# First values of the forward scans: one reciprocal of twelve columns for three limited ones of four, and the copy for the check on ScalarE

## The chip, the cores and the metric

The kernel runs on one core of a Trainium2 chip. The metric is the device time of one execution in microseconds. Engines are named as in the profile: PE (TensorE, matrix products), DVE (VectorE), ACT (ScalarE), POOL (GpSimd) and SP, whose queue issues most of the DMA transfers. An engine works through its own instructions in order; where it needs a result of another engine it waits on a semaphore.

## The reference

A gated linear attention feeds a SoLU block. All data are float32 except the weights of the second block, which come as float64.

```python
B, H, S, D = 4, 8, 768, 48
for t in range(S):
    state = alpha[:, :, t, :, None] * state + einsum('bhd,bhe->bhde', k[:, :, t], v[:, :, t])
    y[:, :, t] = einsum('bhd,bhde->bhe', q[:, :, t], state)
x = y.transpose(0, 2, 1, 3).reshape(3072, 384)
h = x @ w_in                          # 384 x 1024
solu = h * softmax(h)
ln = (solu - mean) / sqrt(var + 1e-6) * g_ln
out = ln @ w_out                      # 1024 x 384
```

alpha lies between 0.8 and 1.0.

## The kernel before

**Groups.** The sequence is cut into G = 6 groups of 128 positions; a group holds all four batches (512 tokens). In each group the attention is computed in chunk form: for position s within a group, the products of alpha up to and from s are put into q and k, so that scores, masked values and the state become matrix products.

**Layout.** For these products alpha, q and k lie with features on partitions: 32 rows per batch, and 12 column blocks (NB = 12): eight blocks, one for each head's first 32 features, and four for the last 16 features of two heads each. A block of alpha has 129 columns (SW = P + 1), the first of which is a zero that separates one block's scan from the next. The 12 blocks are worked in three parts of four (NP = 4, part i = 0, 1, 2; part 2 holds the last features).

**The scans.** Both run on DVE as tensor_tensor_scan (line 220), with state = data0 * state + data1.

- `scan_back(g, i)` runs backward over a part of aT with `unit` (1 in the first column of a block, else 0) and writes hT: the products of alpha from a position to the group's end. Column 1 of a block is then the product over the whole group.
- `scan_on(g, i)` runs forward over a part of aT, in place, with `seed`, which has the inverse of that whole product in the first column of a block and zeros elsewhere. It yields the factors that belong to q.

Before the change, every `scan_on` first limits the four whole products from below by LEAST = 1e-13 into `least` (line 234), takes their reciprocals into a seed tile (line 235) and scans. There are two seed tiles, taken by i % 2. With i = 2, which is the first of a group's three, the 12 whole products are also copied by DVE to `fend` (line 231); at the end of the kernel fend is compared with LEAST, and where any is below, a general path is run instead of this one.

**Who reads the results.** hT is read by the products for keys (kT: by DVE in lines 685 and 762 for groups 0 and 1, by POOL in line 244 from group 2 on) and by `decay` on POOL (line 264). The forward scan's aT is read by the products for queries (qe, qv: lines 693, 772, 780 on DVE; line 255 on POOL from group 2 on). ACT multiplies qe by a parity mask into the second half of qv (`apart`, line 248). The scores (line 282) need kT and both halves of qv; DVE masks them (line 293); the results y (line 314) are copied by ACT to x (line 351).

**The second block.** For each of eight pieces f of 128 features: three accumulated products h (line 389) on PE, exponential on ACT (403), h * e on DVE (404), square on ACT (405), running sums p on POOL and DVE (420). The down projection o (line 500) of one group is interleaved with the attention of a later one; `finish` (517 to 533) forms the row factors with DVE and POOL and writes out.

**Order.** The order of instructions is written out by hand (`tc.manual_schedule()`), and a tile framework places the semaphores. Group 0 and 1 have an order of their own: group 0's transposes are made by PE, and the float64 weights are fetched into a room of slots (`fetch`, line 564, 16 transfers for two pieces of w_in) and unpacked to float32 by DVE (`bits`, lines 594 to 606) beside it. In group 1's attention the three `scan_on` are spread between finish(0) and the query products. Group 2's first two scans stand before group 1's second block, its third in the step behind piece 1 (plan `first`, entry `on1`). For groups 3 to 5 all three stand behind piece 1 of the second block of the group two before:

```python
behind={0: "states v keys", 1: "load on2 on0 on1", 2: "lasts firsts", 3: "apart", 5: "decay", 6: "alpha", 7: "back"},
```

`ps_a` has four PSUM banks of one buffer each, through which transposes, scores, y and the sums pass in turn; `ps_h` and `ps_o` have two each.

Of the kernel before, what the change touches and what calls it, by code (L numbers as in the profile page):

```python
# [9 lines left out]
FP = mybir.dt.float32  # L10
# [4 lines left out]
ALU = mybir.AluOpType  # L15
AX = mybir.AxisListType
P = 128
# [15 lines left out]
def fast_path(ctx, tc, q, k, v, alpha, moe_w_in, moe_w_out, moe_g_ln, out):  # L33
# [12 lines left out]
    nc = tc.nc  # L46
# [5 lines left out]
    NP = H // 2  # L52
    NB = H + NP
# [5 lines left out]
    LEAST = 1e-13  # L59
    PS = bass.MemoryType.PSUM  # L60

    def pool(name, bufs, **kw):
        return ctx.enter_context(tc.tile_pool(name=name, bufs=bufs, **kw))

    const = pool("const", 1)
# [3 lines left out]
    small = pool("small", 4)  # L69
# [27 lines left out]
    fend = const.tile([P, G, NB], FP, name="fend")  # L97
# [19 lines left out]

    SW = P + 1
    aT = const.tile([P, NB, SW], FP, name="aT")
    seed = [const.tile([P, NP, SW], FP, name=f"seed{i}") for i in range(2)]  # L120
    unit = const.tile([P, NP, SW], FP, name="unit")
    hT = const.tile([P, NB * SW + 2], FP, name="hT")
    h4 = hT[:, 0 : NB * SW].rearrange("p (j s) -> p j s", s=SW)
# [92 lines left out]
    def scan(out, data, start, flip):  # L216
        a, o, s = (x.rearrange("p j s -> p (j s)") for x in (data, out, start))
        if flip:
            a, o, s = a[:, ::-1], o[:, ::-1], s[:, ::-1]
        nc.vector.tensor_tensor_scan(out=o, data0=a, data1=s, initial=1.0, op0=ALU.mult, op1=ALU.add)  # L220
# [5 lines left out]

    def scan_on(g, i):
        part = slice(NP * i, NP * i + NP)
        s = seed[i % 2]
        if i == 2:  # L230
            nc.vector.tensor_copy(out=fend[:, g], in_=h4[:, :, 1])

        least = small.tile([P, NP, 1], FP, name="least")
        nc.vector.tensor_scalar(out=least, in0=h4[:, part, 1:2], scalar1=LEAST, scalar2=None, op0=ALU.max)  # L234
        nc.vector.reciprocal(out=s[:, :, 0:1], in_=least)
        scan(aT[:, part], aT[:, part], s, False)

    def keys_T(g):
        firsts(kn, kT[:, 0:H])
# [414 lines left out]
    nc.gpsimd.memset(unit[:, :, 0:1], 1.0)  # L654
    nc.gpsimd.memset(aT[:, :, 0:1], 0.0)
    nc.gpsimd.memset(hT[:, NB * SW : NB * SW + 2], 1.0)
    for s in seed:
        nc.gpsimd.memset(s, 0.0)
    nc.gpsimd.memset(state, 0.0)
    load_v_first(0)  # L660
    fetch(0, 3, 2)
# [18 lines left out]
    turned(kn, ends_of(kn), t)  # L680
    alpha_over(0)
    scan_on(0, 2)
    for i in range(3):
        part = slice(NP * i, NP * i + NP)
        nc.vector.tensor_tensor(out=kT[:, part], in0=t[i], in1=hk[:, part], op=ALU.mult)
    scan_on(0, 0)
    t = three("tp_q", [(ps_o, "o"), (ps_o, "o"), (ps_a, "a0")])
    turned(qn, ends_of(qn), t)
    for i in (2, 0, 1):
        if i == 1:  # L690
            scan_on(0, i)
        part = slice(NP * i, NP * i + NP)
        nc.vector.tensor_tensor(
            out=qe if i == 2 else qv[:, part], in0=t[i], in1=aT[:, part, 1:SW], op=ALU.mult
        )
        if i == 2:
            apart()
# [61 lines left out]
    for i in range(3):  # L759
        scan_back(1, i)  # L760
        part = slice(NP * i, NP * i + NP)
# [15 lines left out]
    for i in range(2):  # L777
        scan_on(1, i)
        part = slice(NP * i, NP * i + NP)
# [150 lines left out]
    def compare(out, x, bound, op):  # L930
# [6 lines left out]
        out=chunks[:, :, 2], in0=sums[:, :, 2], scalar=0.25, in1=sums[:, :, 3], op0=ALU.mult, op1=ALU.is_le  # L937
# [6 lines left out]
    else:  # L944
# [9 lines left out]
        out=bad, in0=all_ok[0:1, 0:1], scalar1=float(P * ends[-1]), scalar2=None, op0=ALU.is_lt  # L954
# [415 lines left out]
def kernel(tc, *args):  # L1370

    with ExitStack() as ctx:
        taken = fast_path(ctx, tc, *args)
    with tc.If(taken > 0):
        general_path(tc, *args)
# [30 lines left out]
```

## Time and profile before

| What | Value |
|---|---|
| Time, median of 7 runs | 391.03 us (389.18 to 394.36) |
| Time of the profiled execution | 390.95 us |
| Span of the profiled execution, first to last instruction | 389.0 us |
| Mean granted TensorE clock in it | 0.991 of full |
| DVE busy, instructions | 250.4 us, 417 |
| ACT busy, instructions | 144.1 us, 252 |
| Forward scans (aT from aT and seed) | 18, 23.0 us |
| least / seed reciprocal / fend copy | 18, 6.5 us / 18, 3.2 us / 6, 2.4 us |

In a row of the timeline stand the start in us from the span's start, the duration in us, the engine, the line of the kernel, the operation, output and inputs with their shape, and the count; in brackets the idle time of the engine just before and what ended it. Rows of a pipelined engine overlap a little. In the list of waits stand the total in us, how often, and the longest. A chain of waits goes back from the last instruction to what released it.

### The profile page before, as it was taken

To read this page: it belongs to the slowest core of one execution; us is meant where nothing else is said; L and a number is where in the kernel's file an instruction comes from. 1 tells how busy PE (TensorE), PEld (TensorE's weight loads), DVE (VectorE), ACT (ScalarE), POOL (GpSimd) and SP (SyncE) were. 2 spreads that over 40 slices of the span, in tenths; PEclk is the share of its full clock that TensorE was granted. 3 is DMA by queue.
4 is the path that set the end of the run, shared out by engine and by line. 5 is a ranking of instruction groups with operands and counts; after the bars stand their busy time and mean duration, and the time that the engine had idled before them with its cause. 6 is when DMAs were issued, how large, how long until landed. Compare 5 with 4: busy or idle time off the path is not lost.

```text
span 389.0 us, 10598 instructions
## 1 busy us (share of the span) xinstructions
PE 371.5 (95%) x4661; PEld 224.4 (58%) x4661; DVE 250.4 (64%) x417; ACT 144.1 (37%) x252; POOL 125.6 (32%) x135
## 2 busy tenths in 40 slices
PE   8798999787999999999999999999999999999995
PEld 8685345455665556656556556566555675555552
DVE  0989889996987767793755893665895511444410
ACT  2528775553425325225153225253123231333111
POOL 4020000041032992337413436422635620333210
PEclk9989999999899999999999999999999999999999
DMA  9975989303446300764000763000600000000011
GB/s 186 193 195 152 235 269 163 93 20 86 111 109 87 83 4 2 111 155 102 22 3 22 117 151 100 22 3 22 103 0 22 22 24 2 20 21 21 22 43 48
DMA packets 86567, 30.79 MB, mean 79 GB/s; under 512 B 68072, under 2 KB 84720, under 8 KB 86512
## 3 DMA queue, kind: packets, MB, share of 16 engines
q1 hardware_dynamic: 85488, 29.11, 34.5%
q10 hardware_dynamic: 1024, 0.92, 0.7%
q8 instruction: 38, 0.62, 0.7%
q14 instruction: 17, 0.14, 0.1%
HBM read 25.30 MB, written 4.72 MB: 77 GB/s over the span
## 4 chain that ended last, share of the span: by engine, by line
PE 71%; DVE 12%; SPq 5%; ACT 5%; DMA 4%; issue 2%; ACTq 0%; DVEq 0%
PE o L500 30%; PE h L389 24%; PE y L314 9%; PE a L282 5%; SPq L564 2%; DMA room<-in_moe_w_in_dram 2%; SPq L152 2%; DVE room L404 2%; PE kv L364 1%; ACT sq L581 1%; DVE aT L220 1%; DMA kn<-in_k_dram 1%; DVE top L597 1%; DVE sT L293 1%; DVE hT L220 1%
## 5 line engine op out<-in xcount | busy, mean ns | idle before, releaser
L500 PE MATMUL o<-w_out,room 128*128 128x385 f32 x384 | 135.2, 496 | 1.0 <-DVE least L234 1.0
L389 PE MATMUL h<-x,w_in 128*128 128x512 f32 x288 | 132.2, 598 | 1.3 <-DVE g_col L618 1.2
L500 PEld LDWEIGHTS o<-w_out,room 128*128 128x128 f32 x384 | 72.0, 191 | 58.2 <-issue 16.1
L389 PEld LDWEIGHTS h<-x,w_in 128*128 128x128 f32 x288 | 53.0, 189 | 59.9 <-issue 48.7
L404 DVE TENSOR_TENSOR room<-h,e 128x512 f32<-128x512 f32 x40 | 27.7, 692 | 82.7 <-ACT e L403 82.5
L403 ACT ACTIVATE e<-h 128x512 f32<-128x512 f32 x40 | 23.9, 598 | 104.9 <-PE h L389 104.9
L530 POOL TENSOR_TENSOR r<-sums,mhalf 128x1 f32<-128x1 f32 x20 | 14.3, 716 | 138.6 <-DVE sums L522 138.6
L420 POOL TENSOR_TENSOR p<-p,e 128x512 f32<-128x512 f32 x30 | 41.7, 1391 | 15.7 <-ACT e L403 15.7
L405 ACT ACTIVATE u<-room 128x512 f32<-128x512 f32 x40 | 25.2, 631 | 42.2 <-DVE room L404 42.2
L293 DVE TENSOR_TENSOR sT<-a,mask 128x512 f32<-128x512 f32 x44 | 27.3, 682 | 9.9 <-PE a L282 8.9
L282 PE MATMUL a<-qv,kT 32*128 32x128 f32 x704 | 27.5, 288 | 4.4 <-DVE least L234 2.2
L282 PEld LDWEIGHTS a<-qv,kT 32*128 32x128 f32 x704 | 24.0, 195 | 11.9 <-issue 4.3
L220 DVE TENSOR_TENSOR_SCAN hT<-aT,unit 128x516 f32<-128x516 f32 x18 | 23.0, 1329 | 8.8 <-ACT aT L677 8.7
L420 DVE TENSOR_TENSOR p<-p,u 128x512 f32<-128x512 f32 x30 | 23.1, 771 | 6.5 <-ACT u L405 6.5
L244 POOL TENSOR_TENSOR kT<-kT,hT 128x1024 f32<-128x1024 f32 (+1 forms) x8 | 13.3, 1684 | 43.0 <-DVE kT L195 43.0
L314 PE MATMUL y<-sT,vn 128*32 128x128 f32 x768 | 23.6, 274 | 1.1 <-DVE sT L293 0.5
L220 DVE TENSOR_TENSOR_SCAN aT<-aT,seed 128x516 f32<-128x516 f32 x18 | 23.0, 1277 | 0.6
L314 PEld LDWEIGHTS y<-sT,vn 128*32 128x32 f32 x768 | 20.9, 110 | 3.3 <-issue 2.4
L212 ACT ACTIVATE sq<-an,mone 128x1536 uint8<-128x1536 f32 x12 | 18.8, 1570 | 0.2
L314 PE MATMUL y<-qv,state 32*32 32x128 f32 x960 | 16.8, 277 | 1.0 <-DVE sT L293 0.9
L314 PEld LDWEIGHTS y<-qv,state 32*32 32x32 f32 x960 | 12.1, 103 | 7.9 <-issue 5.4
L532 ACT ACTIVATE o_sb<-o,r 128x384 f32<-128x384 f32 x16 | 9.3, 582 | 18.8 <-POOL r L530 15.6
(141 smaller groups left out, 379.6 us busy)
## 6 DMA issues: line engine op xcount, KB each, us to landing
an<-in_alpha_dram SPq DMA_DIRECT2D x20, 192.0 KB, 4.9
out_dram<-o_sb SPq DMA_DIRECT2D x20, 192.0 KB, 1.9
room<-in_moe_w_out_dram SPq DMA_DIRECT2D x8, 384.0 KB, 4.8
kn<-in_k_dram SPq DMA_DIRECT2D x16, 192.0 KB, 4.1
qn<-in_q_dram SPq DMA_DIRECT2D x16, 192.0 KB, 3.8
vn<-in_v_dram SPq DMA_DIRECT2D x10, 256.0 KB, 3.9
room<-in_moe_w_in_dram SPq DMA_DIRECT2D x16, 128.0 KB, 4.3
kn<-in_k_dram SPq DMA_DIRECT2D x4, 384.0 KB, 5.8
```

Source lines behind the costliest of these rows:

```text
L212: nc.scalar.activation(out=sq, in_=x, func=AF.Relu, scale=sign, bias=mone, accum_out=over[:, g, i : i + 1])
L220: nc.vector.tensor_tensor_scan(out=o, data0=a, data1=s, initial=1.0, op0=ALU.mult, op1=ALU.add)
L282: nc.tensor.matmul(a[b][:, i], lhsT=kT[quarter(b), kb], rhs=qv[quarter(b), qb], start=kb == h, stop=kb != h, tile_position=(32 * b, 0), sk ...
L293: nc.vector.tensor_tensor(out=sT[:, b, half * NP : half * NP + NP], in0=a[b], in1=mask[:, None, :].to_broadcast([P, NP, P]), op=ALU.mult,)
L314: nc.tensor.matmul(y_bank(b)[quarter(r), a], lhsT=lhsT, rhs=rhs, start=(b, r) not in begun, stop=stop, tile_position=(row, 32 * r), skip_g ...
L389: nc.tensor.matmul(h, lhsT=w_in[:, a, f * P : (f + 1) * P], rhs=d["x"][:, a].rearrange("p b t -> p (b t)"), start=(a == 0), stop=(a == KC ...
L403: nc.scalar.activation(out=e, in_=h, func=AF.Exp)
L404: nc.vector.tensor_tensor(out=u, in0=h, in1=e, op=ALU.mult)
L405: nc.scalar.activation(out=u2, in_=u, func=AF.Square)
L420: eng.tensor_tensor(out=p, in0=d[0][i] if f == 1 else p, in1=d[f][i], op=ALU.add)
L500: nc.tensor.matmul(d["o"][:, 0 : DM + 1], lhsT=u_of(g, f)[:, b * P : b * P + P], rhs=w_out[:, f], start=(f == 0), stop=(f == FC - 1), skip ...
L530: nc.gpsimd.tensor_tensor(out=r, in0=s[:, 3:4], in1=mhalf, op=ALU.pow)
```

## The change

The two seed tiles of four blocks become one of twelve. With i = 2, ahead of the group's first forward scan, one reciprocal takes all 12 whole products from hT, without the limit, and writes the first columns of all blocks of the seed; the copy to fend is made by ACT instead of DVE. The scans read their part of the seed. The comparison of fend with LEAST at the end stays. On POOL the seed is cleared by one memset in place of two.

```diff
-    seed = [const.tile([P, NP, SW], FP, name=f"seed{i}") for i in range(2)]
+    seed = const.tile([P, NB, SW], FP, name="seed")
...
     def scan_on(g, i):
         part = slice(NP * i, NP * i + NP)
-        s = seed[i % 2]
         if i == 2:
-            nc.vector.tensor_copy(out=fend[:, g], in_=h4[:, :, 1])
-
-        least = small.tile([P, NP, 1], FP, name="least")
-        nc.vector.tensor_scalar(out=least, in0=h4[:, part, 1:2], scalar1=LEAST, scalar2=None, op0=ALU.max)
-        nc.vector.reciprocal(out=s[:, :, 0:1], in_=least)
-        scan(aT[:, part], aT[:, part], s, False)
+
+            nc.vector.reciprocal(out=seed[:, :, 0:1], in_=h4[:, :, 1:2])
+            nc.scalar.copy(out=fend[:, g], in_=h4[:, :, 1])
+        scan(aT[:, part], aT[:, part], seed[:, part], False)
...
-    for s in seed:
-        nc.gpsimd.memset(s, 0.0)
+    nc.gpsimd.memset(seed, 0.0)
```

The order of instructions on PE, POOL and SP is the same but for the memset. On DVE 42 instructions go and 6 come; on ACT 6 come: in group 0 behind the two passes over alpha (line 212), in group 1 behind the copies of kg (line 303), in group 2 behind the second passes over alpha and ahead of the x copies, in groups 3 to 5 behind o_sb (line 532).

## The prediction

> **What bounds the kernel now.** I read the page first: its engine rows, then the chain that ended last.
>
> ```profile
> PE 371.5 (95%) x4661; PEld 224.4 (58%) x4661; DVE 250.4 (64%) x417; ACT 144.1 (37%) x252; POOL 125.6 (32%) x135
> PE 71%; DVE 12%; SPq 5%; ACT 5%; DMA 4%; issue 2%; ACTq 0%; DVEq 0%
> ```
>
> TensorE is busy 95% of the span and holds 71% of the chain. Since an average hides stages, I next took the list of waits of PE. From 150 to 389 us it is empty: PE runs through. All its waits lie earlier, and these four are on steps that the touched scans feed (columns: us in total, times, longest):
>
> ```profile
> PE a L282 <- DVE least L234: 2.2, 1, 2.2
> PE a L282 <- DVE qv L780: 1.5, 1, 1.5
> PE a L282 <- ACT qv L248: 0.3, 1, 0.3
> PE a L282 <- POOL qv L255: 0.2, 1, 0.2
> ```
>
> So only time saved in groups 0, 1 and 2 (before about 137 us) can reach the end. Groups 3 to 5 have the same DVE instructions, but there PE is the bound.
>
> **What is removed.** Group rows of DVE by line: the six fend copies are 2.4 us busy, the 18 limits (least) 6.5 us, the 18 reciprocals 3.2 us: 12.1 us. Six reciprocals of 12 columns come in. The trace has none: the row of 4 columns is 180 ns. Lower bound 0.18. Upper: the Trainium skill, "VectorE: DVE Perf Modes", section "First, the fixed hardware budget", runs reciprocal as an iterated divide with a repeat count of 8; 8 more columns at 8 cycles of the page's 0.96 GHz are 67 ns, an estimate of 0.25. By the rows, fend with 12 columns (168 ns) against the copy of 1 column (154) says columns cost little; I take 0.19. The difference is 0.06 a group, three times: 0.2 at most. DVE loses about 11 us of busy time in all. What of it counts must be read from three places.
>
> **Group 1 (80 to 88.6 us)** is the cleanest. The DVE timeline there:
>
> ```profile
> 80.26 0.16 DVE L231 COPY fend<-hT 128x12 f32<-128x12 f32 x1
> 80.33 0.17 DVE L234 TENSOR_SCALAR least<-hT 128x4 f32<-128x4 f32 x1
> 80.53 0.18 DVE L235 RECIPROCAL seed<-least 128x4 f32<-128x4 f32 x1
> 80.75 1.23 DVE L220 TENSOR_TENSOR_SCAN aT<-aT,seed 128x516 f32<-128x516 f32 x1
> ...
> 83.67 0.16 DVE L234 TENSOR_SCALAR least<-hT 128x4 f32<-128x4 f32 x1
> 83.87 0.18 DVE L235 RECIPROCAL seed<-least 128x4 f32<-128x4 f32 x1
> 84.09 1.33 DVE L220 TENSOR_TENSOR_SCAN aT<-aT,seed 128x516 f32<-128x516 f32 x1
> ...
> 86.06 0.24 DVE L234 TENSOR_SCALAR least<-hT 128x4 f32<-128x4 f32 x1
> 86.33 0.18 DVE L235 RECIPROCAL seed<-least 128x4 f32<-128x4 f32 x1
> 86.55 1.29 DVE L220 TENSOR_TENSOR_SCAN aT<-aT,seed 128x516 f32<-128x516 f32 x1
> ```
>
> Instructions that need nothing of the one before start 0.08 before its end; dependent ones 0.02 to 0.03 after it. First scan: the reciprocal runs 80.26 to 80.45, the scan starts at 80.47 instead of 80.75: 0.28. Second and third need no step of their own: 83.68 for 84.09 is 0.41, 86.06 for 86.55 is 0.49. Sum 1.18. The scores of PE start at 88.62, 0.04 after the last qv product (L780), which frees their bank; the down projection ahead of them ends at 86.7, so PE can follow by the whole amount. Late next would be the alpha of group 2 (the SP queue issues it after the ACT pass over alpha, itself after o_sb and a POOL power): I expect it some 0.6 earlier only, but DVE has idle time of 1.3 and 2.0 us before its products at 115.9 and 119.7, which covers it. **1.2 us.**
>
> **Group 0 (13 to 28 us).** By the same counting the three scans start 0.36, 0.76 and 1.23 earlier, PE's scores (19.76) 0.76 earlier, and the masks with them. Behind the eight masks DVE unpacks the first weights (L594, at 27.79), and these need all 16 transfers of the first fetch. The chain shows the issues: the sixteenth at 24.93; its landing takes 2.4 us: 27.33. So from there on DVE gains 27.79 - 27.33 = 0.46 and no more. The second fetch (issued until 33.6, landing about 2.5 later) is needed at 37.4 and doesn't cap further. **0.45 us.** Lower end 0, if the landing moves; upper end 0.76, if it comes earlier.
>
> **Group 2 (119 to 137 us).** On the path is only the third scan; the other two (110 to 113.6) lie ahead of DVE's idle 1.3 us. Here a rule speaks against the plain sum. The rows:
>
> ```profile
> 119.71 1.28 POOL L420 TENSOR_TENSOR p<-e 128x512 f32<-128x512 f32 x1 [4.98 <-ACT e L403]
> 120.27 0.74 DVE L234 TENSOR_SCALAR least<-hT 128x4 f32<-128x4 f32 x1
> 121.04 0.18 DVE L235 RECIPROCAL seed<-least 128x4 f32<-128x4 f32 x1
> 121.26 1.23 DVE L220 TENSOR_TENSOR_SCAN aT<-aT,seed 128x516 f32<-128x516 f32 x1
> ```
>
> The limit took 0.74 instead of its usual 0.16 and ended with POOL's product (120.99). Taken as its own price, limit and reciprocal give back 0.97. But the Trainium skill, "SBUF — State Buffer", section "Who interferes with whom", says that a DVE instruction with two SBUF inputs also blocks behind a GpSimd instruction that reads SBUF. The scan has two (aT and seed), and the row at 110.24 agrees: a scan of 1.88 us while POOL multiplied keys until 111.02. Then the scan, moved to 120.3, waits until 120.99 itself and ends at about 122.2 instead of 122.49. I follow rule and row: **0.3 us**, upper end 0.9. PE could use up to its waits of 0.2 + 0.3 us at 128 to 129 and part of the stall of the scores at 133.8.
>
> **What is added.** The fend copy on ACT: ACT rows near it are 0.19 (128x1) and 0.24 apiece (the state copies of 128x192, four in 0.96); I take 0.2. It is queued behind the two passes over alpha in group 0 (ACT free at 15.2; next is the copy of q's ends, which PE needs at 16.4: 0.5 to spare), ahead of the pair of products by parity in group 1 (ends at about 85, PE needs it at 87.4), and behind o_sb in groups 3 to 5, where ACT idles 2.07 us before the next exponential. In group 2 it adds a true wait: the x copies (105.92 on) stand behind it, and it waits for the last backward scan, ending at 105.5. It is in time by 0.2; and the x copies are needed by PE only at 112.0 (the last ends at 109.9), so the scan may be 2 us late before a microsecond costs one. Nothing. The next group's backward scan must now wait for the copy; that lies four or more steps earlier. The seed memset on POOL grows from 2 x 516 to 1548 columns: at the 1.83 us of vn's 2080 that is 1.36 for 0.99, done at 4.6, needed at 13.3; POOL idles 15 us after it. Nothing moves between queues but this copy; no DMA changes.
>
> **Sum:** 0.45 + 1.2 + 0.3 = 1.95 us. The profiled execution took 390.95 us (span 389.0), close to the median 391.03. 390.95 - 1.95 = **389.0 us**, 0.5% less. A measurement of this kernel tells about 1% from no change, so this counts as within.
>
> **Rivals.**
> - *Nothing arrives* (390.7): the landing caps group 0 wholly, and the alpha of group 2, or POOL's decay (83.8 to 88.7) holds back group 1. For it: DMA has 4% of the chain. Against: the idle times named above. 0.17.
> - *More arrives* (386.6): group 2 gives 0.9, and a half-speed window of PE goes. The table of stretches gives PE a clock of 0.50 from 20.37 to 23.78 and from 98.88 to 102.29, after stretches in which PE was busy 1.21 and 2.42 of 3.41 us; the down projection at 98.6 took 4.55 for the usual 2.8. With shorter waits of PE such a window may not come: 1.95 + 0.6 + 1.75 = 4.3. 0.17.
> - *Slower*, by the same gate: the Trainium skill, "TensorE: Matmul & The Clock Gate", section "Part 1: The HAM clock gate", has the clock follow a free-running activity window of about 3.4 us. By it an earlier PE meets other windows, and where small matmuls (the 32x32 reads, 95 to 108 and later) and a wait fill one, the next runs at half. Each costs 3.41/2 = 1.7 us where PE is the bound. From two additional windows it outweighs the gain: 389.0 + 3.4 = 392.4. By the row alone (two windows stay as they are) it is zero. Against it: waits get shorter, none longer. 0.10; over 1% needs four windows.
> - The forecast has the remaining 0.56, its own range 387.9 to 390.0.
>
> The range 386.9 to 391.6 takes in nothing-arrives, most of more-arrives and a single additional window. Faster by over 1% (below 387.0) is the greater part of the second rival: 0.12; slower by over 1%: 0.06; within: 0.82.
>
> **What would show it.** Right: DVE about 10 us less busy; the scan of group 1's third part begins right with the end of the product before it; the PE wait on qv (1.5) falls to about 0.6 or so; the weight unpacking starts near 27.3 with a DVE idle before it; the third scan of group 2 lasts near 1.9. Wrong: an ACT fend copy that ends after PE has waited for x; a PE wait after 150 us; or more stretches at clock 0.50 than two.

## The result and the profile after

The changed kernel takes 388.54 us (median of 26 runs, 385.88 to 391.48); the kernel before took 393.08 in the 63 runs beside it. Some executions of a kernel show a lower granted clock and take over 1.5% longer than its fastest; they are left out of the ratio and of all means below, so that what is said here of the clock holds for the others alone. The ratio is 0.9911 of before, interval 0.9891 to 0.993, or about 3.5 us less (2.7 to 4.3). The profiled execution took 389.44 us, its span is 387.5.

The engine row of the page after:

```profile
PE 368.2 (95%) x4661; PEld 220.6 (57%) x4661; DVE 245.4 (63%) x381; ACT 144.5 (37%) x258; POOL 125.4 (32%) x134
```

DVE has 36 instructions fewer but is only 5.0 us less busy, though limits, reciprocals and copies made up 12.1. Two rows of the groups (busy us, mean ns, idle us before) say where most of it went:

```profile
L220 DVE TENSOR_TENSOR_SCAN aT<-aT,seed 128x516 f32<-128x516 f32 x18 | 27.2, 1540 | 0.2
L231 DVE RECIPROCAL seed<-hT 128x12 f32<-128x12 f32 x6 | 1.5, 243 | 0.1
```

The forward scans were 23.0 us, 1277 ns each: they are now 4.2 us longer busy, and the new reciprocals add 1.5; the other 1.4 us were not traced. The longer scans stand beside POOL's work: all three of group 2 (2.41, 2.14 and 1.80 us in single records, where they took 1.88, 1.23 and 1.23), and one in each of the groups 3 to 5 (2.23 for 1.23). In group 3 of before it was a limit that took that time, 1.17 us instead of 0.16; after the change the three scans follow each other and share a row:

```profile
166.30 1.17 DVE L234 TENSOR_SCALAR least<-hT 128x4 f32<-128x4 f32 x1
```

```profile
164.72 4.51 DVE L220 TENSOR_TENSOR_SCAN aT<-aT,seed 128x516 f32<-128x516 f32 x3
```

The reciprocal of twelve columns takes 0.22 to 0.23, once 0.33.

**Group 1.** The DVE timeline after:

```profile
83.52 0.22 DVE L231 RECIPROCAL seed<-hT 128x12 f32<-128x12 f32 x1
83.77 1.23 DVE L220 TENSOR_TENSOR_SCAN aT<-aT,seed 128x516 f32<-128x516 f32 x1
...
86.69 1.23 DVE L220 TENSOR_TENSOR_SCAN aT<-aT,seed 128x516 f32<-128x516 f32 x1
...
88.56 1.23 DVE L220 TENSOR_TENSOR_SCAN aT<-aT,seed 128x516 f32<-128x516 f32 x1
```

The second and third scan start right at the end of the product before them. From the start of the first step to the start of the third scan it is 5.04 us, where it was 86.55 - 80.26 = 6.29. PE sees that; its list of waits after:

```profile
PE h L386 <- DVE g_col L615: 4.2, 1, 4.2
PE a L279 <- DVE qv L689: 1.5, 1, 1.5
PE a L279 <- DVE qv L776: 0.4, 1, 0.4
PE a L279 <- ACT qv L245: 0.3, 1, 0.3
```

The wait on group 1's last qv product fell from 1.5 to 0.4, the one in group 0 from 2.2 to 1.5. A new one stands on top: 4.2 us ahead of the first h.

**Group 0.** The last masks and the first unpacking on DVE, the first h on PE, and PE's row in the table of stretches (stretch, busy, granted clock, DMA share, GB/s):

```profile
24.49 1.28 DVE L290 TENSOR_TENSOR sT<-a_o,mask 128x512 f32<-128x512 f32 x2
28.64 0.95 DVE L591 TENSOR_SCALAR top<-room 128x768 uint32<-128x768 uint32 x1 [2.87 <-DMA room<-in_moe_w_in_dram]
```

```profile
33.32 5.18 PE L386 MATMUL h<-x,w_in 128*128 128x512 f32 x6 [4.19 <-DVE g_col L615]
```

```profile
27.85:31.26 3.41, 1.28 (x12) 1.00 0.87 237
31.26:38.09 6.83, 4.77 (x6) 0.50 0.51 127
```

The masks end at 25.8, 2 us earlier than before (1.2 of them because the 64 scores took 2.07 us where they took 3.29 at half clock in the profile of before), and DVE then waits 2.87 us for the first fetch of weights. It unpacks at 28.64, later than the 27.79 of before. PE idles meanwhile, and the 6.83 us after that run at half clock: the first h takes 5.18 us where it took 2.81. This is not the change's doing: kernels with the old form of group 0 show the same start, as the experiments will show.

**Group 2.** POOL's product and the third scan, then ACT's copy and the x copies behind it:

```profile
119.63 1.27 POOL L417 TENSOR_TENSOR p<-e 128x512 f32<-128x512 f32 x1 [3.08 <-ACT e L400]
```

```profile
120.20 1.80 DVE L220 TENSOR_TENSOR_SCAN aT<-aT,seed 128x516 f32<-128x516 f32 x1
```

```profile
108.06 0.21 ACT L232 COPY fend<-hT 128x12 f32<-128x12 f32 x1 [3.03 <-DVE hT L220]
108.17 1.62 ACT L348 COPY x<-y 128x384 f32<-128x384 f32 x4
```

The scan starts as soon as it can and lasts 1.80 instead of 1.23. It ends at 122.00, 1.1 us after POOL's product (120.90), as if it had stood still nearly until then. The new wait on ACT is there: the copy waited for the last backward scan and the x copies stood behind it. They end at 109.8; PE takes x at 111.8.

**Groups 3 and 4.** PE has no listed wait from 150 us on, before or after. Yet its 64 matmuls of the first scores in group 3 changed. The PE timeline of before, and of the whole change:

```profile
182.21 2.78 PE L282 MATMUL a<-qv,kT 32*128 32x128 f32 x64
```

```profile
182.01 2.07 PE L279 MATMUL a<-qv,kT 32*128 32x128 f32 x64
```

The same number of matmuls takes 0.71 less. In group 4 it is 2.66 and 2.07, in group 5 2.07 both times. These stalls make no line in the list of PE's matmuls. The chain of before had them, as four matmuls that together take 0.65 us and then sixty in 2.05:

```profile
182.28 0.65 PE a L282 x4
182.93 2.05 PE a L282 x60
```

The timeline of the weight loads (PEld) of before even names what ended the stall, the copies of kg on ACT; after the change the 64 loads are one row without it:

```profile
182.93 1.86 PEld L282 LDWEIGHTS a<-qv,kT 32*128 32x128 f32 x60 [0.20 <-ACT kg L303]
```

### The profile page after: what moved, and what is told of

Same layout as the page of the kernel before. It is cut to its first block, busy times and chain, and to the rows that moved or that the text cites. A ratio compares the mean times of both kernels' runs of the same rounds, so it can differ in the third digit from the quotient of the medians.

```text
span 387.5 us, 10567 instructions
## 1 busy us (share of the span) xinstructions
PE 368.2 (95%) x4661; PEld 220.6 (57%) x4661; DVE 245.4 (63%) x381; ACT 144.5 (37%) x258; POOL 125.4 (32%) x134
## 4 chain that ended last, share of the span: by engine, by line
PE 67%; DVE 16%; DMA 6%; SPq 4%; ACT 4%; issue 2%; POOL 0%; DVEq 0%; ACTq 0%
PE o L497 28%; PE h L386 24%; PE y L311 7%; PE a L279 4%; SPq L152 3%; DVE aT L220 3%; DMA room<-in_v_dram 2%; DVE room L401 2%; DVE hT L220 2%; DMA kn<-in_k_dram 2%; DVE top L594 1%; SPq L561 1%; DVE aT L195 1%; DMA an<-in_alpha_dram 1%; PE kv L361 1%
## 5 line engine op out<-in xcount | busy, mean ns | idle before, releaser
L386 PE MATMUL h<-x,w_in 128*128 128x512 f32 x288 | 134.5, 607 | 4.2 <-DVE g_col L615 4.2
L497 PE MATMUL o<-w_out,room 128*128 128x385 f32 x384 | 133.5, 491 | 0.8 <-DVE o_mean L523 0.8
L241 POOL TENSOR_TENSOR kT<-kT,hT 128x1024 f32<-128x1024 f32 (+1 forms) x8 | 14.2, 1795 | 43.7 <-DVE kT L195 34.6
L279 PEld LDWEIGHTS a<-qv,kT 32*128 32x128 f32 x704 | 22.0, 186 | 9.5 <-issue 4.7
L279 PE MATMUL a<-qv,kT 32*128 32x128 f32 x704 | 25.0, 278 | 2.4 <-DVE qv L689 1.5
L220 DVE TENSOR_TENSOR_SCAN aT<-aT,seed 128x516 f32<-128x516 f32 x18 | 27.2, 1540 | 0.2
L311 PEld LDWEIGHTS y<-qv,state 32*32 32x32 f32 x960 | 12.1, 103 | 7.9 <-issue 5.4
```

What stands on the lines that cost most here:

```text
L279: nc.tensor.matmul(a[b][:, i], lhsT=kT[quarter(b), kb], rhs=qv[quarter(b), qb], start=kb == h, stop=kb != h, tile_position=(32 * b, 0), sk ...
L311: nc.tensor.matmul(y_bank(b)[quarter(r), a], lhsT=lhsT, rhs=rhs, start=(b, r) not in begun, stop=stop, tile_position=(row, 32 * r), skip_g ...
L386: nc.tensor.matmul(h, lhsT=w_in[:, a, f * P : (f + 1) * P], rhs=d["x"][:, a].rearrange("p b t -> p (b t)"), start=(a == 0), stop=(a == KC ...
L497: nc.tensor.matmul(d["o"][:, 0 : DM + 1], lhsT=u_of(g, f)[:, b * P : b * P + P], rhs=w_out[:, f], start=(f == 0), stop=(f == FC - 1), skip ...
```

## The experiments

Every kernel is built on the changed one, unless said otherwise, and was timed beside before on the same chip, in three sets on three chips. Of each I give the ratio and, since PE's half-speed windows come and go between executions, also the means over the compared runs of the time, of the loss to the clock ((1 - mean granted clock) x span) and of the rest. The rest is a rough measure: it takes off the whole cost of a window even where PE would have waited anyway, and by the scatter of the runs a difference of two rests is known to about 0.7 us. A group's gain is read from the traces too: by how much the starts of PE's h and o products move against another kernel across that group.

### The new first values in one set of groups

```diff
     def scan_on(g, i):
...
+        if g in (0,):        # or (1,), (2,), (3, 4, 5)
+            if i == 2:
+                nc.vector.reciprocal(out=seed[:, :, 0:1], in_=h4[:, :, 1:2])
+                nc.scalar.copy(out=fend[:, g], in_=h4[:, :, 1])
+        else:
+            if i == 2:
+                nc.vector.tensor_copy(out=fend[:, g], in_=h4[:, :, 1])
+            least = small.tile([P, NP, 1], FP, name="least")
+            nc.vector.tensor_scalar(out=least, in0=h4[:, part, 1:2], scalar1=LEAST, scalar2=None, op0=ALU.max)
+            nc.vector.reciprocal(out=seed[:, part, 0:1], in_=least)
+        scan(aT[:, part], aT[:, part], seed[:, part], False)
```

Group 0:

> The new first values in group 0 alone; groups 1 to 5 keep limit, reciprocal and copy on DVE. Theory (DVE path of early groups): between a gain of 0.45 us and nothing, because the unpacking of the weights waits for the first fetch; the changed kernel's profile even shows a loss there (PE idle for 4.2 us before the first h, then h at half clock). Rival (the gain comes from fewer half-speed windows of PE in the start): 1.5 to 2 us faster by itself.

Group 1:

> The new first values in group 1 alone. Theory: 1.2 us faster than before (0.3%), PE's wait on the last qv product 1.5 -> about 0.5. Rival (gain by half-speed windows in the start): no difference, under 0.5 us.

Group 2:

> The new first values in group 2 alone. Theory: 0.3 us faster (0.1%), since the third scan blocks behind POOL's product as the limit did and lasts about 1.8 us. If port blocking were only of the limit: 0.9 us faster, with a scan of 1.23 us.

Groups 3 to 5:

> The new first values in groups 3, 4 and 5 alone. Theory: nothing (within 0.3 us), PE is the bound there and has no waits. Rival (DVE time saved anywhere counts): half of the 11 us of DVE busy time is here, so about half of the measured 3.5 us.

| New in | Ratio (interval) | Time | Loss to the clock | Rest |
|---|---|---|---|---|
| none (before) | 1 | 391.7 | 3.2 | 388.5 |
| group 0 | 1.0064 (1.0037 to 1.0091) | 394.4 | 4.5 | 389.9 |
| group 1 | 0.9981 (0.995 to 1.0013) | 390.5 | 3.1 | 387.4 |
| group 2 | 0.9993 (0.9967 to 1.0019) | 391.7 | 3.3 | 388.4 |
| groups 3 to 5 | 0.999 (0.9966 to 1.0014) | 391.4 | 4.1 | 387.3 |

By the ratio only group 0 is clear of 1, and on the wrong side. The rest, from which the loss to the clock is taken, says more: 1.1 us less for group 1, as the theory had it, and 1.2 less for groups 3 to 5, where it had nothing. The 0.1 of group 2 is too small to be told from 0.3. The traces agree. With group 1 alone PE's products move by 1.3 us across that group, with group 2 alone by 0.5 across group 2 (against the kernels with group 0 and with groups 3 to 5 alone, whose profiles start alike). The first scores of group 3, with group 1 alone and with groups 3 to 5 alone:

```profile
179.64 2.70 PE L285 MATMUL a<-qv,kT 32*128 32x128 f32 x64
```

```profile
188.22 2.07 PE L285 MATMUL a<-qv,kT 32*128 32x128 f32 x64
```

So the stall goes when the group itself has the new first values. Group 2 alone: the third scan takes 1.80, as if behind POOL, and not 1.23:

```profile
125.32 1.80 DVE L220 TENSOR_TENSOR_SCAN aT<-aT,seed 128x516 f32<-128x516 f32 x1
```

### All groups but the first

```diff
-        if g in (0,):
+        if g:
```

> The new first values in groups 1 to 5; group 0 keeps limit, reciprocal and copy on DVE. If group 0's part costs time (it measured +0.64% alone), this is faster than the whole change: about 1.5% below before, 387 us where before is 393. If the parts don't add up because group 0 alone was slow by its own accident, it equals the whole change: 0.991 within 0.2%.

0.9894 (0.986 to 0.9928). Mean 388.4, loss 2.7, rest 385.6. The whole change, once more on the same chip:

> The whole change once more, on the same chip as its neighbours. 0.991 of before as measured first; by the sum of the four parts alone (+0.64, -0.19, -0.07, -0.10%) it would be 1.003.

0.9893 (0.9858 to 0.9928). Mean 388.5, loss 2.7, rest 385.8. The two are equal, so the second forecast came and not the 1.5%, and the whole change is no sum of its parts' ratios: inside it group 0's part gives nothing and costs nothing that can be measured. The cost that it showed alone doesn't carry over. Before itself had a rest of 389.6 in this set, about 1 more than in the other two, so the sums of parts can't be tested to a microsecond by these means.

The start of the changed kernel's profile, with DVE waiting for the fetch and then h at half clock, isn't the change's doing. The kernel with the new first values in groups 3 to 5 alone, whose group 0 is the old one, starts the same way:

```profile
28.11 0.95 DVE L597 TENSOR_SCALAR top<-room 128x768 uint32<-128x768 uint32 x1 [1.86 <-DMA room<-in_moe_w_in_dram]
```

```profile
32.78 5.46 PE L392 MATMUL h<-x,w_in 128*128 128x512 f32 x6 [3.17 <-DVE g_col L621]
```

Of the fourteen profiles (before, after, and one of each experiment), ten have DVE wait 1.86 to 3.53 us for this fetch, five of them with the old form of group 0. The unpacking starts between 28.07 and 28.98 in these five and between 28.20 and 29.68 in the five with the new form. In the other four (before, group 1 alone, all groups but the first, and the second profile of group 0 alone) a half-speed window at about 20 us holds the scores and masks back, and DVE has next to no wait. In the last of these, which has the new form, the unpacking starts at 27.93, and at 27.79 to 27.93 in the three with the old. So the fetch binds the start in five of the eight profiles with the old form as well, and what the new form saves there only lengthens DVE's wait. Whether the new form moves the landing itself can't be told from ranges that overlap.

The profile of the kernel without group 0's part meets the one of before with the same start (a half-speed window at about 20 us, first h at 32.60 and 32.45 at full clock), so these two can be compared step by step. PE's products move by 1.25 us across group 1, 0.44 across group 2, 0.7 at the first scores of group 3 and 0.6 at those of group 4: 3.0 in sum. The spans differ by 4.2, since before had another half-speed window at 98.88, worth 1.7; what is left is small shifts both ways. What ended the stall in group 3 is seen on ACT, in before and then in this kernel:

```profile
179.63 0.58 ACT L532 ACTIVATE o_sb<-o,r 128x384 f32<-128x384 f32 x1 [3.22 <-DMA qn<-in_q_dram]
180.11 1.32 ACT L248 ACTIVATE qv<-qe,parity 128x512 f32<-128x512 f32 x2
181.33 1.55 ACT L303 COPY kg<-tp 128x512 f32<-128x512 f32 x3
```

```profile
175.72 0.58 ACT L535 ACTIVATE o_sb<-o,r 128x384 f32<-128x384 f32 x1 [3.21 <-POOL r L533]
176.20 1.32 ACT L251 ACTIVATE qv<-qe,parity 128x512 f32<-128x512 f32 x2
177.43 1.54 ACT L306 COPY kg<-tp 128x512 f32<-128x512 f32 x3
```

The copies of kg read three PSUM banks that the scores write next. In before the copies end at 181.90, 182.39 and 182.88 (single records of the row of three). The scores into the first bank start at 182.21, when PE is done with the work ahead. Those into the second start at 182.44 and those into the third at 182.93, each 0.05 us after the copy of its bank. Here the last copy ends at 178.97 and the scores start at 179.38, unhindered. All profiles agree: with the old first values in groups 3 and 4 (seven profiles, fourteen cases) the scores run on 0.05 us after the last copy; with the new ones (the other seven) the copies have ended 0.41 to 0.53 before the scores start. Group 5 has no copies of kg, and neither a stall nor a gain. Behind DVE's scans come the query transposes, POOL's products, POOL's power for the row factor, o_sb, the parity products and the copies: relative to PE, 1.1 us saved at the top arrive at the bottom, where 0.7 were wanted. No run moved the copies by themselves; that the bank is the link rests on these times and on the order of the code.

### Which of the two edits

One reciprocal without limit, the copy left on DVE, in all groups:

```diff
-            nc.scalar.copy(out=fend[:, g], in_=h4[:, :, 1])
+            nc.vector.tensor_copy(out=fend[:, g], in_=h4[:, :, 1])
```

> One reciprocal of 12 columns without the limit, the fend copy stays on DVE in all groups. Theory: the copy is 0.08 us of DVE's path in group 1 (80.26 to 80.33), so nearly all of the gain stays: within 0.1% of the whole change. Rival (it is ACT's copy that matters, by POOL's port, as where the copy lasted 1.58 us in group 2): most of the gain is lost.

0.9929 (0.9895 to 0.9963). Mean 389.7, loss 3.6, rest 386.1: the rest is 0.3 above the whole change, the remainder of the difference is the clock. By the ratio the 0.1% that was expected can be neither confirmed nor denied, since the intervals of the two overlap; that most of the gain would be lost is ruled out. The copy alone on ACT, limits and reciprocals kept:

```diff
         if i == 2:
-            nc.vector.reciprocal(out=seed[:, :, 0:1], in_=h4[:, :, 1:2])
             nc.scalar.copy(out=fend[:, g], in_=h4[:, :, 1])
+        least = small.tile([P, NP, 1], FP, name="least")
+        nc.vector.tensor_scalar(out=least, in0=h4[:, part, 1:2], scalar1=LEAST, scalar2=None, op0=ALU.max)
+        nc.vector.reciprocal(out=seed[:, part, 0:1], in_=least)
```

> Only the fend copy goes to ACT; every scan keeps its limit and reciprocal on DVE. Theory: 0.1 us on the path of group 1, nothing elsewhere: no difference (within 0.2%). Rival (the copy's blocking behind POOL is what costs): half of the gain or more, 0.995.

0.9992 (0.9963 to 1.0021), as the theory had it. The first scores of group 3, with the reciprocal alone and with the copy alone:

```profile
184.77 2.07 PE L279 MATMUL a<-qv,kT 32*128 32x128 f32 x64
```

```profile
184.77 2.70 PE L280 MATMUL a<-qv,kT 32*128 32x128 f32 x64
```

The gain is that of the limits and reciprocals. The copy, which lasted 1.58 us on DVE in group 2 of before, was not on the path.

### The clock

The changed kernel with 14 matmuls of constants ahead of the first h:

```diff
     keys_back(0)
+    warm(14)
     in_range(0)
```

> The whole change with 14 matmuls of constants (about 3 us, results unused) on PE behind the transposes of group 0's keys, where PE idles before the first h. Theory (that idle time of 4.2 us makes the two half-speed windows at 31 to 38 us): the windows go, up to 3 us faster than the whole change (0.8%). Rival (the start is bound by the landing of the weights and DVE, not by PE): no gain, or 1 us slower by the added work.

0.9923 (0.9887 to 0.9958), 11 runs. In its profile the added matmuls fill the idle time (each float32 product has two records, as the three of h have six); the timeline of PE and its stretches:

```profile
29.25 3.29 PE L442 MATMUL warm<-ones 128*128 128x128 f32 x28
33.24 2.81 PE L386 MATMUL h<-x,w_in 128*128 128x512 f32 x6 [0.70 <-DVE g_col L615]
```

```profile
27.85:31.26 3.41, 3.41 (x31) 1.00 0.80 231
31.26:38.09 6.83, 6.13 (x116) 1.00 0.44 105
```

The half clock is gone there and h takes 2.81 again. The mean loss fell to 2.0 us, but the rest rose to 386.3, and the mean time, 388.3, is that of the whole change (388.5), though the ratio is a little higher than its 0.9893: no gain is shown. With eight such matmuls and the old form of group 0:

> The new first values in groups 1 to 5 and 8 matmuls of constants (1.8 us) ahead of the first h. If half-speed windows in the start cost time in either form of group 0: up to 1.5 us faster than without the matmuls (388 where that was 389). If the landing of the weights binds the start: the same within 0.2%.

0.9883 (0.9836 to 0.993), mean 387.2 in 6 runs, loss 2.0, rest 385.2. It is the lowest of all, yet its interval contains those of the whole change and of the kernel without group 0, which ran on another chip; a better version is not shown.

The kernel before with 6 matmuls in group 1's wait:

```diff
     down(2, 0)
+    warm(6, ps_h, "h")
     scores(1, 0)
```

> The kernel before, with 6 matmuls of constants (1.3 us, results unused) on PE in group 1, between the down projection and the scores, where PE waits 1.48 us for the last qv product. Theory (this wait makes the half-speed windows at 93 to 97 and 103 to 107 us that several executions of before-like kernels show, and the whole change gains by shortening it): 1 to 2 us faster than before with nothing else changed, and few runs with a mean clock under 0.983. Rival (the windows come from the small matmuls of the reads, whatever the wait): no faster, or slower by up to 0.3 us.

0.9999 (0.9965 to 1.0033); loss 3.4, against 3.1 for before in that set. The mean clock was never under 0.983, as the theory had it, but in the 42 runs of before beside it that came only twice. That group 1's wait costs 1 to 2 us by the clock is not borne out: filling the wait without shortening it gives no gain, or at most 1.4 us by the interval.

### Group 0 alone, once more

> The new first values in group 0 alone, once more. If its 0.64% is the part's own cost, it shows again (1.005 or more); if it came of that set of runs, 1.000 within 0.2%, as the start of its profile says (first h 0.3 us from the one of the kernel with groups 3 to 5 alone).

1.0029 (0.9984 to 1.0074); loss 3.8, rest 389.0 against 388.7 for before. In both sets 0.5 us of it lie outside the span: time less span is 2.4 us for this kernel and 1.9 to 2.0 for all others. Of the 2.7 us by which the means of the first set differ, 1.2 were clock and 0.5 lay outside the span; the remaining 0.9 didn't come again. Why this program alone has more time outside the span was not tried, and so its own cost is left open.

## Why the prediction was right or wrong

The time forecast, 389.0, is 0.5 us from the median measured, and within 1% held, though the second measurement, 0.9893, lies just beyond it. That the time came so close is partly luck. The forecast started from 390.95; beside the changed kernel before took about 392.1, by the ratio. The saving was forecast as 1.95 and is about 3.5 by the ratio, whose interval of 2.7 to 4.3 leaves the forecast out, and 3.0 by the steps of the traces.

- **Group 1, 1.2 us:** right. 1.25 to 1.3 by the traces. The steps forecast as 0.28, 0.41 and 0.49 came as 0.24, 0.42 and 0.59; the wait on qv fell to 0.4, forecast 0.6.
- **Group 2, 0.3:** the mechanism was right, the size 0.44. The scan blocked behind POOL as the limit had done (1.80, forecast 1.9), which the plain price of the removed rows would have missed. Here the rule of the Trainium skill, "SBUF — State Buffer", section "Who interferes with whom", on two SBUF inputs decided rightly: the third scan lasts 1.80 in all seven profiles with the edit in group 2.
- **Group 0, 0.45:** nothing that can be measured. The cap by the landing was seen, but the 0.46 between it and DVE came from one execution, in which a half-speed window had held the masks back. In five of the eight profiles with the old form of group 0 DVE waits for the fetch already, 1.86 to 2.82 us. The lower end of 0 was the better value.
- **Groups 3 to 5, nothing:** the step that failed. "From 150 to 389 us it is empty: PE runs through" was read from the list of waits of PE's matmuls, and that list doesn't hold a stall inside a run of matmuls of one line. Two stalls of 0.71 and 0.59 stood in the durations of PE's own rows, in the chain, and in the timeline of the weight loads, which names the copies of kg. The prediction itself knew a stall of this kind, that of the scores at 133.8 in group 2, and didn't look for it behind 150. The two are 1.3 us, more than the 1.05 by which the steps of the traces exceed the forecast, since group 0 gave less.
- **DVE about 10 us less busy:** 5.0. The limits' 6.5 us had much waiting for POOL in them, and the waiting passed on to the scans.
- **ACT's copy at nothing:** right. 0.20 to 0.23 us each, and in group 2 a wait of 3.0 us that stayed covered.
- **The rival of more gain:** the saving of about 3.5 lies nearer to its 4.3 than to the forecast, but neither of its two causes is shown. Group 2 gave 0.44 and not 0.9, and the loss to the clock is 3.2 and 2.7 us in the two sets of the changed kernel and 3.1 to 3.2 in those of before, where it is known. The slower rival didn't come.

## What to carry to other kernels

When an engine seems to run through, compare the durations of equal runs of its instructions, not only its waits: 64 equal matmuls in 2.78 us here and in 2.07 there are a stall, though the list of PE's waits had no line for it. Look at the waits of the weight loads too. Count an instruction that had been waiting for another engine by what the next one will then wait for: of the 1.35 us that the second limit and reciprocal of group 3 took, 1.0 came back in the row of the scan. Where an edit runs up against a transfer, take its landing from more than one execution, and see whether the execution at hand is a usual one.

## What the runs showed of the hardware that I had not expected

Half-speed windows of PE last 3.41 us or twice that, apart from one that runs into the end of the kernel, and in the first 40 us the fourteen profiles show two kinds of start, with the old form of group 0 and with the new. Four have one window, from 19.76 to 20.63 us on, and the first h, at 32.45 to 32.60, takes 2.81. Eight have a double one, from 31.26 to 33.13 on, and the first h, at 32.8 to 34.4, takes 5.18 to 5.46. The two with added matmuls ahead of h have none there. The windows follow stretches of 3.41 us in which PE had little to do (1.21 us busy in before, 1.28 after), but also stretches busy for 2.42, with many 32x32 matmuls among them.

The cost of a window depends on what is behind it. With the early one the masks come late, and still the unpacking starts at 27.79 to 27.93, earlier than in any other profile; the next h products start at 36.7 to 36.8. With the double one, which falls on the first h, they start at 39.8 to 41.3. So profiles of two kernels can be compared step by step only if they start alike. That filling one such gap with work lowers the loss but not the time, within the interval, was new to me.
